# Residual adds, q rests, gradient stores and normalized-input stores moved between engines and queues in a one-core transformer-block backward kernel

## The chip, the cores and the metric

The kernel runs on one core of one Trainium2 chip. A core has TensorE (PE, matmuls and the loads of their stationary operand, PEld), VectorE (DVE), ScalarE (ACT), GpSimd (POOL) and SyncE (SP), each with an instruction stream of its own that runs in order, and DMA queues that SyncE, ScalarE and GpSimd issue to. The metric is the device time of one execution in microseconds (us); lower is better.

## The reference

One pre-norm block is run forward, and the gradients of all its inputs are taken. Everything is bf16, S = 2048 tokens, D = 640, H = 32 heads of 20, F = 1728.

```python
def _A_ref(x, wqkv, wo):                       # linear attention
    q, k, v = split_heads(x @ wqkv)
    phi = lambda t: jnp.where(t > 0, t + 1, jnp.exp(t)) + 1e-6
    pq, pk = phi(q), phi(k)
    kv = jnp.einsum("bhsd,bhse->bhde", pk, v)
    z = jnp.einsum("bhsd->bhd", pk)
    o = jnp.einsum("bhqd,bhde->bhqe", pq, kv) / (jnp.einsum("bhqd,bhd->bhq", pq, z)[..., None] + 1e-6)
    return join_heads(o) @ wo

def _B_ref(x, w1, w3, w2):                     # gated MLP
    return (silu(x @ w1) * (x @ w3)) @ w2

h = x + _A_ref(layernorm(x), wqkv, wo)
out = h + _B_ref(layernorm(h), w1, w3, w2)
# outputs: out, and the gradients of x, wqkv, wo, w1, w3, w2 for a given grad_out
```

## The kernel before, in words

Tokens are cut into 16 tiles of 128 rows (`t`), grouped four to a chunk of 512 (`c`); F is cut into 14 slices of 128 (`fc`), taken in pairs (`k`). The order of instructions on every engine is the order in which the Python code emits them (a manual schedule); the framework only adds the waits. Tile pools recycle their buffers, so a write to a recycled buffer waits for whatever still reads it. DMAs of one queue are handed out over eight semaphores in turn, so one also waits for the eighth before it.

The work goes through these stages:

1. **Start, about 0 to 78 us.** x is loaded and normalized tile by tile in place (`ln1`, `x_sb`); TensorE transposes the first eight tiles, and DMA transposes (`p1_norm`) make `pqT` for the others. Each tile gets k (`p1_mm`, `phi`) and some tiles q. The function phi is split: ScalarE computes exp and relu from the accumulator (`mq`, `rq`), and a held "rest" on VectorE (min, add, add) finishes it later (`phi_rest` runs held rests in order, leaving `keep` of them). A list `trickle` holds loads of weights, of which one is issued per tile; `group_out` stores a finished group of four k tiles (`pk_d`) and normalized x tiles (`xn_d`). `load_wq` loads 320 columns of wqkv per step, `load_w2T` loads w2 transposed, and `ghh_chunk` multiplies it with grad_out ahead of need.
2. **Attention output, about 78 to 107 us.** A hand-written list of steps (`run((q_late, 10, f2_mT), ...)`) interleaves: the last q tiles 10 to 15 (`q_late`), the product of kv and wo (`f2_wT`), the division by the denominator (`r_...`), the attention output plus the residual for tiles 0 to 4 (`f2_half(t, j)`, j being a half of 320 columns), the statistics of the second norm (`ln2.part`), the normalized tile (`f2_hn`) and its transpose on TensorE (`f2_ht`). By the time the residual is added, x_sb has been reloaded with x.
3. **Gated MLP, about 107 to 336 us.** For each chunk and slice, TensorE computes `ghh` (four slices ahead), gate and up; ScalarE moves them out of PSUM (L668 to L676); after every pair, seven VectorE products (`mlp_pair`, `op`) are queued in `later` and drained one at a time. Three of them are stored to DRAM by `store`: hh, and the gradients of gate and up (`gg_d`). The tiles sig, s2, gate and up have two buffers each, so ScalarE's copy into `up` of pair k + 2 waits until the store of pair k has landed. Side steps (`sides`, `r_steps`) compute the attention output of the next chunk and the scaled q rows (`r_load`, `r_den`, `r_end`).
4. **Gradients, from 355 us.** Weight gradients, input gradients and their norms; they read back what was stored.

`f2_at` adds the residual in one of two ways. For tiles 5 to 7, TensorE adds it with a matmul of the identity and x, and ScalarE copies the sum into x_sb; for all others, VectorE adds accumulator and x_sb:

```python
on_pe = TPC < t < 2 * TPC
...
    if on_pe:
        T.matmul(at[:, 0:HD], lhsT=ident[:], rhs=xs, start=True, stop=False)
...
    if on_pe:
        A.copy(out=xs, in_=at[:, 0:HD])
    else:
        V.tensor_tensor(out=xs, in0=at[:, 0:HD], in1=xs, op=ALU.add)
```

GpSimd computes the reciprocal square root of each variance (`ln_rs`, L152) and issues stores of the q rows (`r_d`, `pq_d`) and of a few small matrices.

Of the kernel before, what the change touches and what calls it, by code (L numbers as in the profile page):

```python
# [9 lines left out]
P = 128  # L10
BF16 = mybir.dt.bfloat16
F32 = mybir.dt.float32
ALU = mybir.AluOpType
# [11 lines left out]
HD = D // 2  # L25
# [30 lines left out]
def kernel(  # L56
# [116 lines left out]
    wqkv = U1.tile([P, DT, 3 * D], BF16, name="wqkv", tag="D")  # L173
    wq_v = A_wqkv.rearrange("(c p) n -> p c n", p=P)

    def load_wq(a, b, q=dma):
        q(out=wqkv[:, :, a * HD:b * HD], in_=wq_v[:, :, a * HD:b * HD])

    def load_x(a, b):
        dma(out=x_sb[:, a:b, :], in_=xS[:, a:b, :])  # L180

    load_x(1, 2)
    A.activation(sg[:], zero[:], AF.Exp)
    load_wq(2, 3, A.dma_start)
    load_wq(3, 4, A.dma_start)
    load_x(2, 3)
    load_x(3, 4)
    load_x(4, 6)
# [229 lines left out]
    load_w2T(0, 2 * P)  # L418
    load_x(6, 8)
    load_g2T(0)  # L420
    load_x(8, 12)
    load_wq(0, 2)
    load_x(12, ST)
# [10 lines left out]
        ln1.part(x_sb, t + 1, 0)  # L434
        p1_norm(t)
    ln1.part(x_sb, 3, 1)
    trickle += [lambda: load_w2T(2 * P, 4 * P), lambda: load_wq(4, 6)]
    for c0, c1 in ((0, 2), (2, 4), (4, 5)):
        trickle += load_w13(c0, c1)
    trickle += [lambda: dma(out=w1[:, :, F:FP], in_=rows(B_w3)[:, :, F - FL:F])]  # L440
# [4 lines left out]
    stat_of = {0: (4,), 1: (5,), 2: (6,), 3: (7,), 4: (8, 9), 5: (10,), 6: (11,), 7: (12, 13), 8: (14,), 9: (15,)}  # L445
    norm_of = {0: (3,), 1: (4,), 2: (5,), 3: (6,), 4: (7,), 5: (8, 9), 6: (10,), 7: (11,), 8: (12, 13), 9: (14,), 10: (15,)}

    def group_out(g):
        sl = slice(g * TPC, (g + 1) * TPC)
        dma(out=pk_v[:, sl, :], in_=pk_all[:, sl, :])  # L450
        dma(out=xn_v[:, sl, :], in_=x_sb[:, sl, :])

    QT = (5, 7, 9, 11)
    for t in range(ST):
# [98 lines left out]
    hn, hnT, hhT = {}, {}, {}  # L553

    def f2_at(t, tag="at", halves=(0, 1)):
        on_pe = TPC < t < 2 * TPC
        for j in halves:
            at = ps.tile([P, 512], F32, name="at", tag=tag, bufs=2)
            xs = x_sb[:, t, j * HD:(j + 1) * HD]
            if on_pe:  # L560
                T.matmul(at[:, 0:HD], lhsT=ident[:], rhs=xs, start=True, stop=False)
            for c in range(DT):
                T.matmul(at[:, 0:HD], lhsT=pqT[:, c, t * P:(t + 1) * P], rhs=Wp[:, c, j * HD:(j + 1) * HD],  # L563
                         start=(c == 0 and not on_pe), stop=(c == DT - 1))
# [3 lines that stand above are left out]
                V.tensor_tensor(out=xs, in0=at[:, 0:HD], in1=xs, op=ALU.add)  # L568
            ln2.part(x_sb, t, j)

    def q_late(t, between=None):

        mq, rq = (p1.tile([P, D], BF16, name=n, bufs=b) for n, b in (("mq", 3), ("rq", 3)))
        q_home(t)
        for j in range(2):
            acc = ps.tile([P, 512], F32, name="mm", bufs=4)
            js = slice(j * HD, (j + 1) * HD)
            p1_half(acc[:, 0:HD], t, j * HD)
            if j == 0 and between is not None:
                between()  # L580
            A.activation(mq[:, js], acc[:, 0:HD], AF.Exp)
            A.activation(rq[:, js], acc[:, 0:HD], AF.Relu)

# [21 lines left out]
    def f2_mT():  # L605
        tr = ps.tile([P, DT, P], BF16, name="trm", tag="at", bufs=2)
        for c in range(DT):
            T.transpose(tr[:, c, :], mbs[:, 0, c * P:(c + 1) * P], ident[:])
        A.copy(out=mT[:, :, (DT - 1) * P:], in_=tr[:])

    def q_out(a, b):
        src = pq6[:, 4:6, :] if a == 8 else pkx[0][:, DT + a - 10:DT + b - 10, :]
# [67 lines left out]
        if i == 1:  # L680
            mlp_pair(c, k, *pair.pop(k), ghh.pop(n // 2))

    def store(dst, r0, c, k, src):
        cs = slice(c * W, (c + 1) * W)
        r0 += k * 2 * P
        if k < FT // 2 - 1:
            dma(out=dst[r0:r0 + 2 * P, cs].rearrange("(i p) w -> p i w", p=P), in_=src)
        else:
            dma(out=dst[r0:r0 + P, cs], in_=src[:, 0, :])
            dma(out=dst[r0 + P:r0 + P + FL, cs], in_=src[:FL, 1, :])  # L690

    later = []

# [4 lines left out]
    def mlp_pair(c, k, sig, s2, gate, up, gh):  # L698

        hh = hhT[c][:, 2 * k:2 * k + 2, :]  # L700

        def op(out, a, b, alu=ALU.mult, to=None, r0=0):
            def go():
                V.tensor_tensor(out=out, in0=a, in1=b, op=alu)
                if to is not None:
                    store(to, r0, c, k, out)
            later.append(go)

        sig, s2, gate, up, gh = (x[:] for x in (sig, s2, gate, up, gh))
        op(gate, gate, sig)  # L710
        op(hh, gate, up, to=hh_d)
        op(s2, gate, s2)
        op(gate, gate, gh, to=gg_d, r0=F)
        op(s2, s2, sig, ALU.add)
        op(s2, s2, up)
        op(up, s2, gh, to=gg_d)

    def o2_steps(c, q=dma, tag="o2"):

# [33 lines left out]
    def run(*steps):  # L753
# [3 lines left out]
    Wp = U1.tile([P, DT, D], BF16, name="Wp", tag="MW")  # L757
    pkx.append(p1.tile([P, DT + 6, D], BF16, name="pkx", tag="pk"))
    run((q_late, 10, f2_mT), (f2_kv, 2), (f2_kv, 3), (f2_kv, 4), (phi_rest,), (q_late, 11), (f2_wT, 0), (f2_wT, 1),
        (phi_rest,), (q_late, 12), (f2_wT, 2), (f2_wT, 3), (f2_wT, 4), (phi_rest,), (q_late, 13),  # L760
        (r_red, 3), (r_inv, 3), (r_scale, 3), (r_prod, 5), (load_x, 2, 4), (r_T, 3), (q_late, 14), (r_red, 4),
        (r_inv, 4), (r_scale, 4), (r_T, 4), (load_x, 4, 8), (mlp_ghh, 4), (load_w2T, 8 * P, 10 * P), (q_late, 15),
        (sig_table,), (f2_half, 0, 0), (f2_half, 1, 0), (f2_half, 0, 1), (f2_half, 1, 1), (f2_hn, 0), (mlp_ghh, 5),
        (f2_half, 2, 0), (f2_hn, 1), (f2_m_out,), (load_w2T, 10 * P, 12 * P), (f2_half, 2, 1), (phi_rest, 2),
        (f2_ht, 0), (mlp_ghh, 6), (f2_half, 3, 0), (f2_hn, 2), (f2_w_out,), (f2_ht, 1), (f2_half, 3, 1), (phi_rest, 1),
        (mlp_ghh, 7), (f2_half, 4, 0), (f2_hn, 3), (phi_rest,), (q_out, 10, 16), (load_w2T, 12 * P, F), (f2_ht, 2),
        (f2_ht, 3), (f2_half, 4, 1), (r4_out,), (r_red, 5), (r_inv, 5), (r_scale, 5), (r_out, 5), (r4b_out,),
        (q_out, 8, 10))
    p1.release()
    pa = pool("pa", "right")  # L770

# [25 lines left out]
    def r_end(t):  # L797
# [1 line left out]
        r_out(t)  # L799

    r_steps = [{1: ((r_den, 6),), 2: ((r_end, 6), (r_load, 8)), 4: ((r_den, 7), (r_load, 9)), 5: ((r_end, 7),),
                12: ((r_load, 10),)},
               {0: ((r_den, 8),), 1: ((r_end, 8), (r_load, 11)), 2: ((r_den, 9),), 3: ((r_end, 9), (r_load, 12)),
                5: ((r_den, 10),), 6: ((r_end, 10), (r_load, 13)), 8: ((r_den, 11),), 9: ((r_end, 11), (r_load, 14)),
                11: ((r_den, 12),), 12: ((r_end, 12), (r_load, 15))},
               {0: ((r_den, 13),), 1: ((r_end, 13),), 3: ((r_den, 14),), 4: ((r_end, 14),), 6: ((r_den, 15),),
# [1 line left out]
    for c in range(SC):  # L808
        hhT[c] = pa.tile([P, FT, W], BF16, name="hhT", bufs=2)
        o2 = o2_steps(c - 1) if c > 0 else None  # L810

        def run_side(pos, fc):
            if c + 1 < SC:
                for f, i in sorted(sides[c][pos].get(fc, ()), key=lambda x: (x[0] is f2_ht, x[1])):
                    f((c + 1) * TPC + i)

        for fc in range(FT):
            mlp(c, fc, lambda: run_side(0, fc))
            drain(1)
            if o2 and not (c == SC - 1 and fc == 5):  # L820
                next(o2, None)
            run_side(1, fc)
            drain(1)
            if (c, fc) in ((0, 12), (1, 2)):
                load_x(8 + 4 * c, 12 + 4 * c)
            if c == 0 and fc in (5, 7, 9, 11):
                a, b = {5: (0, 3), 7: (3, 6), 9: (6, 10), 11: (10, 13)}[fc]
                dma(out=w2[:, a:b, :], in_=B_w2[a * P:b * P, :].rearrange("(c p) n -> p c n", p=P))
                if fc == 11:
                    dma(out=w2[0:FL, FT - 1, :], in_=B_w2[(FT - 1) * P:F, :])  # L830
            for f, t in r_steps[c].get(fc, ()):
                f(t)
# [569 lines left out]
```

## Time and profile before

| What | Value |
|---|---|
| time, median of 4 runs | 839.91 us (838.47 to 843.01) |
| profiled execution: time | 838.47 us |
| profiled execution: span, first to last instruction | 836.8 us |
| mean granted TensorE clock | 0.998 |
| TensorE busy | 820.7 us (98%) |
| VectorE busy | 456.3 us (55%) |
| ScalarE busy | 316.9 us (38%) |
| GpSimd busy | 79.7 us (10%) |
| mean DMA rate | 188 GB/s |

A row of the timeline gives the start and the time taken in us from the span's start, then the engine ("SPq" is SyncE's sequencer, which issues DMAs), the line in the kernel, the operation and the tiles; in brackets stands how long the engine was idle before it, and what released it. A row of the costliest groups gives the busy time, the mean of one in ns, and the idle time before them. TensorE is an in-order engine whose matmuls are pipelined: five of 320 columns take about 0.68 us, five of 512 about 1.08 us.

### The profile page before, as it was taken

Reading aid. Unit: us, or ns where it says so; the run is one execution under the profiler, and the core shown is the slowest. Engines: PE = TensorE matmul, PEld = TensorE weight load, DVE = VectorE, ACT = ScalarE, POOL = GpSimd, SP = SyncE. Lnnn points to the kernel's source line nnn. Section 1 sums busy time; section 2 is a strip of 40 time slices with the busy share of each in tenths; the row PEclk is TensorE's granted clock in tenths of the full one; section 3 lists DMA queues with packets and bytes.
Section 4 is the critical chain, followed back from the end, with each engine's and each line's share of the span. In section 5 each row is a group of like instructions: output and inputs, shape, how many; then the busy total and the mean of one; then the engine's idle time right before and its main releaser. Section 6 shows DMA issues by size and latency. Waiting matters only on the chain.

```text
span 836.8 us, 14163 instructions
## 1 busy us (share of the span) xinstructions
PE 820.7 (98%) x5548; PEld 523.9 (63%) x5548; DVE 456.3 (55%) x968; ACT 316.9 (38%) x599; POOL 79.7 (10%) x117
## 2 busy tenths in 40 slices
PE   8999899999999999999999999999999999999998
PEld 5667544455555555777777777777777777555554
DVE  7947988798998666500037777772681545200000
ACT  5755657755555666111122121222211433311111
POOL 2314221001010000000001111110110000000000
PEclk9999999999999999999999999999999999999999
DMA  9998978685585357799967788436998798876671
GB/s 265 261 350 148 219 238 216 205 226 152 144 202 156 111 162 219 205 240 226 287 159 178 191 188 209 96 89 124 207 243 173 162 190 178 214 186 149 158 172 37
DMA packets 330066, 157.58 MB, mean 188 GB/s; under 512 B 235344, under 2 KB 327152, under 8 KB 330000
## 3 DMA queue, kind: packets, MB, share of 16 engines
q1 hardware_dynamic: 302000, 136.61, 67.5%
q10 hardware_dynamic: 25728, 12.05, 6.7%
q0 software_dynamic: 2272, 8.03, 2.8%
q8 instruction: 43, 0.70, 0.4%
q14 instruction: 23, 0.19, 0.1%
HBM read 48.15 MB, written 51.46 MB: 119 GB/s over the span
## 4 chain that ended last, share of the span: by engine, by line
PE 88%; DVE 4%; DMA 3%; ACT 1%; SPq 1%; issue 1%; DVEq 0%; ACTq 0%
PE job L1167 19%; PE mm L364 19%; PE ghn L969 14%; PE o L728 7%; PE gxn L1326 7%; PE gw L922 7%; PE gwo L1054 3%; PE gr L1026 3%; PE macc L385 2%; PE dkv L1270 2%; PE big L255 2%; PE at L563 2%; DMA w2T<-in_B_w_dram 1%; DMA pqT<-x_sb 1%; DVE st L147 1%
## 5 line engine op out<-in xcount | busy, mean ns | idle before, releaser
L1167 PE MATMUL job<-gb,hnN 128*128 128x432 bf16 x640 | 117.0, 346 | 0.0
L969 PEld LDWEIGHTS <-ggb 128*128 128x128 bf16 x864 | 84.5, 98 | 32.8
L1167 PEld LDWEIGHTS <-hnN 128*128 128x128 bf16 x640 | 62.6, 98 | 54.1
L364 PE MATMUL mm<-pqT,w 128*128 128x512 bf16 x405 | 94.3, 381 | 0.0
L364 PEld LDWEIGHTS <-w 128*128 128x128 bf16 x540 | 53.1, 98 | 63.5 <-issue 0.8
L1171 ACT CAST obs<-job 128x432 bf16<-128x432 f32 (+1 forms) x60 | 29.1, 485 | 123.6 <-PE job L1167 121.2
L728 PE MATMUL o<-w,hhT 128*128 128x320 bf16 x448 | 67.5, 299 | 0.0
L364 PE MATMUL mm<-g2T,w2T 128*128 128x512 bf16 x260 | 64.6, 379 | 2.2 <-ACT up L676 2.2
L969 PE MATMUL ghn<-w13a,ggb 128*128 128x320 bf16 x448 | 63.5, 299 | 0.0
L969 PE MATMUL ghn<-w13b,ggb 128*128 128x320 bf16 x416 | 61.4, 299 | 0.0
L728 PEld LDWEIGHTS <-hhT 128*128 128x128 bf16 x448 | 43.8, 98 | 23.6
L922 PE MATMUL gw<-g,hb 128*128 128x320 bf16 x416 | 57.0, 299 | 0.0
L922 PEld LDWEIGHTS <-hb 128*128 128x128 bf16 x416 | 40.6, 98 | 15.7
L374 ACT CAST ghh<-mm 128x512 bf16<-128x512 f32 x52 | 30.6, 588 | 51.1 <-PE mm L364 48.5
L1326 PE MATMUL gxn<-wqT,gT 128*128 128x320 bf16 x320 | 48.9, 299 | 0.1
L1034 POOL TENSOR_TENSOR sz<-Zb,g_h 128x640 f32<-128x640 bf16 x16 | 20.2, 1261 | 270.7 <-issue 162.9
L364 PEld LDWEIGHTS <-w2T 128*128 128x128 bf16 x280 | 27.2, 98 | 28.8 <-issue 2.5
L668 ACT ACTIVATE sig<-mm 128x512 bf16<-128x512 f32 x56 | 33.6, 600 | 29.0 <-PE mm L364 26.5
L255 PE MATMUL big<-wqkv,pqT 128*128 128x320 bf16 x260 | 39.3, 299 | 3.0 <-ACT pqT L251 1.6
L981 ACT ACTIVATE gs<-ghn 128x640 bf16<-128x640 f32 x16 | 11.2, 703 | 78.6 <-PE ghn L969 78.6
L255 PEld LDWEIGHTS <-pqT 128*128 128x128 bf16 x320 | 30.4, 98 | 16.7 <-ACT pqT L251 2.5
L1326 PEld LDWEIGHTS <-gT 128*128 128x128 bf16 x320 | 31.2, 98 | 12.5 <-DMA gT<-g_k 0.4
(186 smaller groups left out, 1222.7 us busy)
## 6 DMA issues: line engine op xcount, KB each, us to landing
hh_d<-hhT SPq DMA_DIRECT2D x24, 256.0 KB, 2.4
gg_d<-gate SPq DMA_DIRECT2D x24, 256.0 KB, 3.0
gg_d<-up SPq DMA_DIRECT2D x24, 256.0 KB, 2.8
ggb<-gg_d SPq DMA_DIRECT2D x6, 896.0 KB, 5.9
ggb<-gg_d SPq DMA_DIRECT2D x6, 832.0 KB, 7.0
out_dram<-obs ACTq DMA_DIRECT2D x40, 108.0 KB, 2.5
ggb<-gg_d SPq DMA_DIRECT2D x2, 1728.0 KB, 12.7
x_sb<-in_A_x_dram SPq DMA_DIRECT2D x5, 640.0 KB, 5.8
```

What stands on the lines that cost most here:

```text
L255: T.matmul(acc, lhsT=pqT[:, c, t * P:(t + 1) * P], rhs=wqkv[:, c, n0:n0 + HD], start=(c == 0), stop=(c == DT - 1))
L364: T.matmul(acc[:], lhsT=w[:, c, fc * P:(fc + 1) * P], rhs=rhs[:, c, :], start=(c == 0), stop=(c == DT - 1))
L374: A.copy(out=ghh[n // 2][:, n % 2, :], in_=acc[:])
L668: A.activation(sig[:, i, :], gp[:], AF.Sigmoid)
L728: T.matmul(o2["ps"][:, 0:HD], lhsT=hhT[c][:, fc, i * P:(i + 1) * P], rhs=w2[:, fc, j * HD:(j + 1) * HD], start=(fc == 0), stop=(fc == FT - 1))
L922: T.matmul(acc[:, j, 0:HD], lhsT=hb[b][:, t, i * P:(i + 1) * P], rhs=g2[:, t, j * HD:(j + 1) * HD], start=(t == 0), stop=(t == ST - 1))
L969: T.matmul(acc[:, j, 0:HD], lhsT=ggb[t // 2][:, k, lo:lo + P], rhs=rhs[:, j * HD:(j + 1) * HD], start=(k == 0), stop=(k == NG - 1))
L1026: T.matmul(gr[t][:, j, 0:HD], lhsT=ghT[t][:, c, :], rhs=wT2[:, c, j * HD:(j + 1) * HD], start=(c == 0), stop=(c == DT - 1))
L1054: T.matmul(acc[m][:, j, 0:n], lhsT=r_sb[:, t, m * P:(m + 1) * P], rhs=g_hx[:, t, j * HD:j * HD + n], start=(t == 0), stop=(t == ST - 1))
L1167: T.matmul(acc[:, 0:n], lhsT=lhs[:, t, m * P:(m + 1) * P], rhs=rhs(t), start=(t == 0), stop=(t == ST - 1))
L1171: A.copy(out=ob, in_=acc[:, 0:n])
L1326: T.matmul(acc[:, j, 0:HD], lhsT=g, rhs=wqT[:, k, j * HD:(j + 1) * HD], start=(k == 0), stop=(k == 14))
```

## The change

There are five edits.

- `f2_at` decides per half: the residual of half j = 1 goes by the identity matmul for tiles below 4 as well. Tile 4 stays with VectorE.
- `q_late` for tiles 14 and 15 writes its exp and relu into a tile `qx` that takes the memory of wo, which is no longer needed then, and finishes in place there. Their rests are run by a new step `q_rest` at slice 4 of MLP chunk 1, which also stores both tiles to `pq_d`; `q_out` in the attention stage stores tiles 10 to 13 alone.
- The hand-written list of steps is reordered a little: `f2_wT(4)` runs between the halves of `q_late(13)`, and the last `phi_rest`, `q_out`, `f2_ht`, `mlp_ghh(7)` and `f2_half(4, 0)` change places.
- The store of the up gradient goes to GpSimd's queue; hh and the gate gradient stay on SyncE's.
- The stores of normalized x of groups 2 and 3 leave `group_out` and are issued by GpSimd in MLP chunk 0, slices 6 and 13; the reload of x_sb tiles 12 to 15 moves from slice 2 to slice 5 of chunk 1. At the start, all wqkv loads go by SyncE, and the second load of w2T leaves `trickle` and is issued ahead of the load of x tiles 8 to 11.

```diff
-    def load_wq(a, b, q=dma):
-        q(out=wqkv[:, :, a * HD:b * HD], in_=wq_v[:, :, a * HD:b * HD])
+    def load_wq(a, b):
+        dma(out=wqkv[:, :, a * HD:b * HD], in_=wq_v[:, :, a * HD:b * HD])
...
-    load_wq(2, 3, A.dma_start)
-    load_wq(3, 4, A.dma_start)
+    load_wq(2, 3)
+    load_wq(3, 4)
...
     load_g2T(0)
+    load_w2T(2 * P, 4 * P)
     load_x(8, 12)
...
-    trickle += [lambda: load_w2T(2 * P, 4 * P), lambda: load_wq(4, 6)]
+    trickle += [lambda: load_wq(4, 6)]
...
+    def xn_out(g, q):
+        sl = slice(g * TPC, (g + 1) * TPC)
+        q(out=xn_v[:, sl, :], in_=x_sb[:, sl, :])
+
     def group_out(g):
         sl = slice(g * TPC, (g + 1) * TPC)
         dma(out=pk_v[:, sl, :], in_=pk_all[:, sl, :])
-        dma(out=xn_v[:, sl, :], in_=x_sb[:, sl, :])
+        if g < 2:
+            xn_out(g, dma)
...
-        on_pe = TPC < t < 2 * TPC
         for j in halves:
+            on_pe = t < 2 * TPC and (t > TPC or (t < TPC and j == 1))
...
-        mq, rq = (p1.tile([P, D], BF16, name=n, bufs=b) for n, b in (("mq", 3), ("rq", 3)))
-        q_home(t)
+        if t < 14:
+            mq, rq = (p1.tile([P, D], BF16, name=n, bufs=b) for n, b in (("mq", 3), ("rq", 3)))
+            q_home(t)
+        else:
+            if t == 14:
+                qx.append(U1.tile([P, DT, D], BF16, name="qx", tag="W6"))
+            mq, rq = (qx[0][:, 2 * (t - 14) + i, :] for i in range(2))
+            pqs[t] = mq
...
+    def q_rest():
+        phi_rest()
+        dmaG(out=pq_v[:, 14:16, :], in_=qx[0][:, 0:4:2, :])
...
-    def store(dst, r0, c, k, src):
+    def store(dst, r0, c, k, src, q):
...
-            dma(out=dst[r0:r0 + 2 * P, cs].rearrange("(i p) w -> p i w", p=P), in_=src)
+            q(out=dst[r0:r0 + 2 * P, cs].rearrange("(i p) w -> p i w", p=P), in_=src)
...
-        op(up, s2, gh, to=gg_d)
+        op(up, s2, gh, to=gg_d, q=dmaG)
...
-        (phi_rest,), (q_late, 12), (f2_wT, 2), (f2_wT, 3), (f2_wT, 4), (phi_rest,), (q_late, 13),
+        (phi_rest,), (q_late, 12), (f2_wT, 2), (f2_wT, 3), (phi_rest,), (q_late, 13, lambda: f2_wT(4)),
...
-        (f2_half, 2, 0), (f2_hn, 1), (f2_m_out,), (load_w2T, 10 * P, 12 * P), (f2_half, 2, 1), (phi_rest, 2),
-        (f2_ht, 0), (mlp_ghh, 6), (f2_half, 3, 0), (f2_hn, 2), (f2_w_out,), (f2_ht, 1), (f2_half, 3, 1), (phi_rest, 1),
-        (mlp_ghh, 7), (f2_half, 4, 0), (f2_hn, 3), (phi_rest,), (q_out, 10, 16), (load_w2T, 12 * P, F), (f2_ht, 2),
-        (f2_ht, 3), (f2_half, 4, 1), (r4_out,), (r_red, 5), (r_inv, 5), (r_scale, 5), (r_out, 5), (r4b_out,),
-        (q_out, 8, 10))
+        (f2_half, 2, 0), (f2_hn, 1), (f2_m_out,), (load_w2T, 10 * P, 12 * P), (f2_half, 2, 1),
+        (f2_ht, 0), (mlp_ghh, 6), (f2_half, 3, 0), (f2_hn, 2), (f2_w_out,), (f2_ht, 1), (f2_half, 3, 1), (phi_rest, 2),
+        (q_out, 10, 14), (f2_ht, 2), (f2_hn, 3), (mlp_ghh, 7), (load_w2T, 12 * P, F), (f2_half, 4, 0), (f2_ht, 3),
+        (f2_half, 4, 1), (r4_out,), (r_red, 5), (r_inv, 5), (r_scale, 5), (r_out, 5), (r4b_out,), (q_out, 8, 10))
...
-                12: ((r_load, 10),)},
-               {0: ((r_den, 8),), 1: ((r_end, 8), (r_load, 11)), 2: ((r_den, 9),), 3: ((r_end, 9), (r_load, 12)),
+                6: ((xn_out, 2, dmaG),), 12: ((r_load, 10),), 13: ((xn_out, 3, dmaG),)},
+               {0: ((r_den, 8),), 1: ((r_end, 8), (r_load, 11)), 2: ((r_den, 9),), 3: ((r_end, 9), (r_load, 12)), 4: ((q_rest,),),
...
-            if (c, fc) in ((0, 12), (1, 2)):
+            if (c, fc) in ((0, 12), (1, 5)):
                 load_x(8 + 4 * c, 12 + 4 * c)
```

More of the change, by code (lines that the diff above doesn't have):

```diff
@@ L569, in f2_at @@
             ln2.part(x_sb, t, j)
+    qx = []
     def q_late(t, between=None):
-        mq, rq = (p1.tile([P, D], BF16, name=n, bufs=b) for n, b in (("mq", 3), ("rq", 3)))
-        q_home(t)
+        if t < 14:
[6 more added lines that the diff above has]
+            pqs[t] = mq
         for j in range(2):
@@ L686, in store @@
         if k < FT // 2 - 1:
-            dma(out=dst[r0:r0 + 2 * P, cs].rearrange("(i p) w -> p i w", p=P), in_=src)
+            q(out=dst[r0:r0 + 2 * P, cs].rearrange("(i p) w -> p i w", p=P), in_=src)
         else:
-            dma(out=dst[r0:r0 + P, cs], in_=src[:, 0, :])
-            dma(out=dst[r0 + P:r0 + P + FL, cs], in_=src[:FL, 1, :])
+            q(out=dst[r0:r0 + P, cs], in_=src[:, 0, :])
+            q(out=dst[r0 + P:r0 + P + FL, cs], in_=src[:FL, 1, :])
     later = []
@@ L700, in mlp_pair, with op @@
         hh = hhT[c][:, 2 * k:2 * k + 2, :]
-        def op(out, a, b, alu=ALU.mult, to=None, r0=0):
+        def op(out, a, b, alu=ALU.mult, to=None, r0=0, q=dma):
             def go():
@@ L705, in go @@
                 if to is not None:
-                    store(to, r0, c, k, out)
+                    store(to, r0, c, k, out, q)
             later.append(go)
@@ L830 @@
                     dma(out=w2[0:FL, FT - 1, :], in_=B_w2[(FT - 1) * P:F, :])
-            for f, t in r_steps[c].get(fc, ()):
-                f(t)
+            for f, *t in r_steps[c].get(fc, ()):
+                f(*t)
             if c == 2 and fc == 3:
```

## The prediction

> **What bounds the kernel now.** I read the page's busy times first, then TensorE's chain of waits, then the timeline where those waits stand.
>
> ```profile
> PE 820.7 (98%) x5548; PEld 523.9 (63%) x5548; DVE 456.3 (55%) x968; ACT 316.9 (38%) x599; POOL 79.7 (10%) x117
> ```
>
> The chain of TensorE's waits (line, waited for: us in total, times, longest):
>
> ```profile
> PE trh L640 <- DVE hn L155: 3.9, 2, 3.0
> PE mm L364 <- ACT up L676: 2.2, 1, 2.2
> ...
> PE gp L364 <- DMA w2T<-in_B_w_dram: 1.0, 1, 1.0
> PE big L255 <- DMA pqT<-x_sb: 0.8, 1, 0.8
> ```
>
> TensorE is busy 820.7 of 836.8 us. Only what shortens its idle 16.1 us, or what is added to its work, can move the time. Two waits are large: 3.9 us behind VectorE's hn, and 2.2 us behind ScalarE's copy into `up`.
>
> ```profile
> 102.10:105.10 3.00, 0.01 (x1) 0.00 (x0) 2.79 (x9) 0.69 (x1) 0.56 (x1) 0.93 0.89 337
> 105.10:108.40 3.30, 3.29 (x15) 1.83 (x16) 1.82 (x5) 0.69 (x1) 0.87 (x1) 0.55 0.66 175
> ```
>
> Two stretches (time, then PE, PEld, DVE, ACT, POOL busy, granted clock, DMA). In the first TensorE does nothing and VectorE is 93% busy: VectorE is the bound from about 85.7 us to hn(3). In the second the granted clock is 0.55. So the wait of 3.0 us is paid a second time: at half clock, 3.3 us hold about 1.65 us of matmul.
>
> ```profile
> 119.71 0.69 DVE L704 TENSOR_TENSOR up<-s,ghh 128x1024 bf16<-128x1024 bf16 x1
> ...
> 120.09 0.57 POOL L358 DMA_DIRECT2D r_d<-pql  x1 [6.41 <-DVE pql L350]
> ...
> 121.75 0.40 SPq L687 DMA_DIRECT2D gg_d<-up  x1
> ...
> 125.98 0.58 ACT L676 CAST up<-mm 128x512 bf16<-128x512 f32 x1 [3.44 <-DMA gg_d<-up]
> ...
> 126.62 1.24 PE L364 MATMUL mm<-g2T,w2T 128*128 128x512 bf16 x5 [2.20 <-ACT up L676]
> ```
>
> The second wait: `up` of pair 0 is finished at 120.40, but its store is issued at 121.75, behind a transpose and a load in SyncE's queue; it lands at 125.88 (4.13 us), ScalarE may then overwrite the tile, and TensorE resumes at 126.62.
>
> **The change part by part.**
>
> *Residuals and q rests.* The rows (busy, mean ns, idle before):
>
> ```profile
> L568 DVE TENSOR_TENSOR x_sb<-at,x_sb 128x320 bf16<-128x320 f32 x26 | 12.5, 482 | 5.1 <-PE at L563 5.1
> ...
> L566 ACT CAST x_sb<-at 128x320 bf16<-128x320 f32 x6 | 2.7, 465 | 0.6 <-PE at L563 0.6
> ...
> L561 PE MATMUL at<-x_sb,ident 128*128 128x320 bf16 x6 | 1.8, 299 | 0.0
> ```
>
> The condition covers four halves (tiles 0 to 3, j = 1), not five: tile 4 meets neither branch. VectorE's timeline from the first L568 (91.85) to the end of hn(3) (105.05) is 13.2 us without a gap that matters. Out of it go four L568, 0.52 from start to start: 2.1. Tile 14's rest (L585, L586: 102.86 to 103.69) goes: 0.8. The add and statistics of tile 4's first half (103.69 to 104.62) now come after hn(3): 0.9. VectorE's own chain becomes 13.2 - 3.8 = 9.4 us. It also starts 0.35 earlier, since tile 12's rest no longer waits behind wT(4) (VectorE idles 0.49 there at 85.73).
>
> By that VectorE would finish at 100.9; but then TensorE and ScalarE bind. TensorE from at(0,0) at 90.69: ten attention halves at 0.68, four identity matmuls at 0.14 (starts 116.15 to 116.29), three ghh chunks at 1.08, four transposed tiles at 0.37 = 6.8 + 0.56 + 3.24 + 1.5 = 12.1, to 102.8. Following each release, I find two stops: at(3,0) ends at 98.5, then bn, hn(2), ScalarE's copy of (3,1) at 99.8 to 100.25 (0.47), its statistics, tile 13's rest (0.8, kept), and hn(3) ends at 102.4, so trh(2) and trh(3) wait about 0.5 together; ScalarE's copy of trh(3) ends at 103.6. The MLP starts at 103.7 instead of 106.95: 3.25 gained, the identity matmuls paid. ScalarE's 1.28 us table load at 91.67 delays copy (0,1) to 93.16, and costs VectorE 0.35 there, which it can spare. No gap near 3 us remains, so the half clock goes as well; before the MLP that is in the 3.25, and from 106.95 to 108.4 it is half of 1.45 = 0.75 more. Together 4.0. Bounds: 2.0 (copies late) to 4.9 (TensorE never waits).
>
> The two rests (two of 0.32 and 0.49, 1.6 us) go to MLP chunk 1, step 4, just ahead of an `up` product near 179.6. VectorE is idle 0.97 before the next pair there, and TensorE has four accumulators of lead; I take 0. Without that cover: 1.6. The data stay in wo's tile, which wT(4) has finished with; the reload of tiles 14 and 15 is at steps 9 and 12 of that chunk, at least 15 us after the new store.
>
> *Up stores on GpSimd.* 24 large stores and 4 split ones leave SyncE's queue. GpSimd has no row for 128x2x512. Its 160 KB stores in the MLP (`r_d<-pql`) take 0.54 to 0.58 to issue and 3.0 to 4.5 to land, 3.1 in the middle; its 320 KB store 0.74 and 3.9. For 256 KB I take 0.65 and 3.6. Behind each in GpSimd's queue stand ln_rs (a later product of VectorE, so already late enough) and r_d stores; r_load waits for those at least one step later.
>
> Take G, the end of gate(1) on ScalarE (112.53 before). VectorE is full from G until `up` is done at G + 7.9. Before, TensorE ran dry at G + 11.85 and resumed at G + 14.1. Now: r_d of tile 6 is issued until G + 8.15, the store lands at G + 11.75, ScalarE's copy takes 0.6, TensorE resumes at G + 12.45: the stop is about 0.55 instead of 2.2, gain 1.7. Some is given back: the next store ends 128.47 + 0.1 + 3.3 to 3.6 = about 132, while ScalarE, now 1.7 earlier, asks at 129.1 (it asked at 130.76). TensorE's lead over ScalarE there is 2.4 to 3.3, so I charge 0.4. Net 1.3; bounds 0 to 2.2. Later pairs: from VectorE's end to ScalarE's next use are 3.5 to 4.9 us in chunks 0 and 1, about the 3.7 that a store takes; the waits of 1.4 and 2.4 us that ScalarE has before at 187.0 and 161.6 cost TensorE nothing, so a small excess is covered.
>
> *The rule against it.* The Trainium skill, "SBUF — State Buffer", section "SBUF: two separate sides" and the one after it, says that VectorE and GpSimd lock one shared pair of ports, so that VectorE's two-port modes keep GpSimd from writing descriptors; it tells of a DMA of 0.62 us that took 3.1 us so. That would add 2.5: landing at 6.1, the first stop 2.95 instead of 0.55, and some 1 us more at the next pairs: about 3 us worse. The row decides for 3.6: the same queue's stores landed in 3.0 to 4.5 with VectorE 94% busy. The lock does show in ln_rs, 0.87 to 0.93 in the MLP against 0.56 ahead of it.
>
> *Loads and xn stores.* Ahead of about 40 us VectorE is full and DMA is too. The wqkv halves move behind x(1) on SyncE; x(1) lands sooner than its 5.19, but VectorE next needs x(2), and x(0..2) plus both halves are 1.31 MB at the 300 GB/s of that stretch: 4.4 + 2.8 = 7.2, as now (7.14). The w2T load ahead of x(8..11) ends the 1.0 us wait of gp, which VectorE hides anyway. x(8..11) then land near 16.9, and VectorE needs them at 18.89. But the trickle is one item ahead: w3's first 0.85 MB (3 us) now stands before pqT(8), the first stores and pqT(10), where DMA had room at 32 to 36 us.
>
> ```profile
> 36.65 2.89 SPq L242 DMA_TRANSPOSE pqT<-x_sb  x2
> ...
> 44.64 1.53 PE L255 MATMUL big<-wqkv,pqT 128*128 128x320 bf16 x10 [0.82 <-DMA pqT<-x_sb]
> ```
>
> That wait ends with the second of these transposes, 6.65 us after its issue at 37.95; I put it 0.6 to 1.1 later, and TensorE has no slack from there to 78 us. I charge 0.8 (bounds: 0.8 gained to 2.0 lost). The two late xn stores (0.66 MB each, GpSimd, chunk 0 at steps 6 and 13) leave a full queue at 44 to 60 us where TensorE does not wait, and precede their overwriting loads by six steps: 0; uncovered, some 2.3 us of DMA each.
>
> **Sum.** 3.25 + 0.75 + 1.3 - 0.8 = 4.5. The profiled execution took 838.47 (span 836.8 and 1.7 around it), so its like is 834.0; it is the fastest of the four runs, whose median is 839.91, so I forecast 835.4.
>
> **Rivals.** (a) All goes well: no loss at the start, TensorE never waits for `up`: 3.25 + 0.75 + 2.2 = 6.2, and the 0.8 us wait gone: 7.0, so 832.9. For it: both waits are near their ends. (b) Descriptors are starved as the skill's page says: 838.4. Against it, the landings quoted. (c) ScalarE is late with the four copies behind table load and ghh casts, the lower bound of 2.0: 837.4. Against it: ScalarE is busy 5.2 of 13.3 us there. (d) The w2T transpose holds SyncE's queue for 5.0 us, as the same transpose did at 12.53; x(8..11) are issued at 16.5 and land near 22, 3 us after VectorE needs them: 838.4. Against it: at 12.53 three loads stood ahead of that transpose, now none. (e) The other side: up stores slower than the buffers bear. With 4 us from VectorE's end to ScalarE's use and 3 of TensorE's lead, landing beyond some 7 us stops TensorE at each pair; at 8 us that is 1 us in 24 pairs: 839.9 - 4.0 + 0.8 + 24 = 861. Against it: 4.5 was the longest.
>
> **How the numbers follow.** Forecast 0.58, own range 833.4 to 837.4; (a) 0.12; (b) 0.08; (c) 0.08; (d) 0.04; (e) 0.10. Half a per cent, about what a measurement of this kernel can tell, puts the bound at 835.7: two thirds of the forecast's case and (a) lie below, 0.39 + 0.12 = 0.51 faster; (e) 0.10 slower; the rest 0.39. The range 832.0 to 839.6 takes in (a) to (d).
>
> **What would show it.** Right: trh waits for hn under 1 us; granted clock 1.0 in the MLP's first 3 us; MLP matmuls from about 104; the wait for `up` under 1.2; `gg_d<-up` from GpSimd landing at 3.2 to 4.2; the wait for pqT near 45 us at 1 to 2. Wrong: TensorE waiting for ScalarE's `x_sb` copies or for `up` more than once, landings over 6, or VectorE waiting for x_sb near 19 us.

## The result and the profile after

The changed kernel takes 837.61 us (median of 43 runs, 835.02 to 840.54) against 839.54 us for the kernel before (64 runs). The ratio is 0.9971, 95% interval 0.9963 to 0.9979: 2.4 us faster, with an interval of 1.8 to 3.1 (the two medians alone differ by 1.9). The forecast was 4.5 us, to 835.4, with 833.4 to 837.4 as the range of its own case; the measured time lies 0.2 us above that range.

The two profiled executions do not show this difference: the one before is a quick one of its kernel (838.47), the one after a slow one (838.87), and their spans are 836.8 and 837.2 us. So the profiles are compared stage by stage here, and times are taken from the medians.

| us | start to first attention half (L563, after L569) | from there to first MLP matmul | MLP, to first `gw` matmul | from there to the end |
|---|---|---|---|---|
| before | 90.68 | 16.27 | 247.89 | 481.91 |
| after | 90.23 | 14.82 | 250.71 | 481.40 |

The MLP starts at 105.05 instead of 106.95: 1.90 gained. Of these, 0.45 came before the first attention half; the stretch behind it, for which 3.25 had been forecast, became 1.45 shorter. Then the MLP is 2.8 us longer. Busy times of the changed kernel:

```profile
PE 820.3 (98%) x5552; PEld 522.9 (62%) x5552; DVE 453.8 (54%) x964; ACT 317.8 (38%) x603; POOL 103.8 (12%) x152
```

VectorE has 2.5 us of work less, GpSimd 24 us more, and TensorE is as busy as before. Its waits in the changed kernel (line, waited for: us in total, times, longest; `trh` is the transpose of hn, `mm` at L364 a product of the MLP):

```profile
PE trh L658 <- DVE hn L155: 2.7, 1, 2.7
PE mm L364 <- ACT up L694: 2.4, 4, 1.1
PE big L255 <- ACT pqT L251: 1.6, 2, 0.8
PE mm L364 <- DMA pqT<-hn: 1.5, 1, 1.5
PE big L255 <- DMA pqT<-x_sb: 1.3, 3, 0.8
```

The wait for hn only fell from 3.9 to 2.7. The wait for `up` is no smaller: one stop of 2.2 became four that sum to 2.4. And one wait is new, 1.5 us for `pqT<-hn`. The timeline of the changed kernel shows what stands behind each. First, the entry to the MLP:

```profile
94.63 2.45 SPq L413 DMA_TRANSPOSE w2T<-in_B_w_dram  x1
...
94.92 0.44 DVE L155 TENSOR_SCALAR hn<-x_sb,ln_mv,ln_rs 128x640 bf16<-128x640 bf16 x1
...
97.18 1.02 SPq L646 DMA_DIRECT2D hn_d<-hn  x2
...
101.28 0.45 DVE L155 TENSOR_SCALAR hn<-x_sb,ln_mv,ln_rs 128x640 bf16<-128x640 bf16 x1 [2.22 <-DMA hn_d<-hn]
...
101.78 0.45 PE L658 MATMUL trh<-ident,hn 128*128 128x128 bf16 x5 [2.69 <-DVE hn L155]
```

hn has two buffers, so hn(2) may be written only when the store of hn(0) has landed. hn(0) is ready at 95.36, but SyncE is in a transposing load of w2T from 94.63 and issues the store at 97.18; it lands at 101.2. VectorE, which has its work done early now, waits 2.22 us for it. Before the change the store was issued as soon as hn(0) was written, landed at 100.90, and hn(2) started at 101.16:

```profile
96.41 0.44 DVE L155 TENSOR_SCALAR hn<-x_sb,ln_mv,ln_rs 128x640 bf16<-128x640 bf16 x1
...
96.88 1.61 SPq L628 DMA_DIRECT2D hn_d<-hn  x2
...
101.16 0.43 DVE L155 TENSOR_SCALAR hn<-x_sb,ln_mv,ln_rs 128x640 bf16<-128x640 bf16 x1
```

So the store was done 0.26 us before VectorE came to hn(2), and no row showed it as a wait.

Second, the third `up` store of MLP chunk 0, same view:

```profile
132.23 0.69 DVE L722 TENSOR_TENSOR up<-s,ghh 128x1024 bf16<-128x1024 bf16 x1
...
132.59 0.79 POOL L451 DMA_DIRECT2D xn_d<-x_sb  x1
133.48 0.71 POOL L705 DMA_DIRECT2D gg_d<-up  x1
139.31 0.58 ACT L694 CAST up<-mm 128x512 bf16<-128x512 f32 x1 [4.15 <-DMA gg_d<-up]
139.94 1.24 PE L364 MATMUL mm<-g2T,w2T 128*128 128x512 bf16 x5 [0.50 <-ACT up L694]
...
140.25 0.89 DVE L147 BATCH_NORM_STATS2 st<-x_sb 128x6 f32<-128x320 bf16 x2 [3.43 <-ACT x_sb L572]
```

One of the two moved xn stores is issued just ahead of an `up` store, which then lands after 5.73 us. ScalarE waits 4.15 us for the buffer; behind its copy of `up` in ScalarE's order stands a residual copy (L572), so VectorE waits 3.43 us for that. TensorE itself stops three more times, by 0.50, 0.28 and 0.55 us. At the boundary of chunks 1 and 2 it stops again, same view:

```profile
215.29 0.44 DVE L155 TENSOR_SCALAR hn<-x_sb,ln_mv,ln_rs 128x640 bf16<-128x640 bf16 x1
...
216.87 1.24 SPq L654 DMA_TRANSPOSE pqT<-hn  x1
...
221.23 2.33 PE L364 MATMUL mm<-pqT,w 128*128 128x512 bf16 x10 [1.47 <-DMA pqT<-hn]
```

The half clock at the start of the MLP is gone in this execution (stretch; PE, PEld, DVE, ACT and POOL busy; granted clock; DMA share and rate):

```profile
99.10:101.78 2.68, 0.00 (x1) 0.01 (x1) 0.50 (x2) 0.42 (x1) 0.00 (x0) 1.00 1.18 350
...
105.05:108.35 3.30, 3.30 (x16) 1.53 (x16) 3.09 (x9) 2.02 (x4) 1.30 (x2) 1.00 0.92 317
```

### The profile page after: what moved, and what is told of

It is laid out like the page before. It is cut to its first block, busy times and chain, and to the rows that moved or that the text cites. A ratio compares the mean times of both kernels' runs of the same rounds, so it can differ in the third digit from the quotient of the medians.

```text
span 837.2 us, 14175 instructions
## 1 busy us (share of the span) xinstructions
PE 820.3 (98%) x5552; PEld 522.9 (62%) x5552; DVE 453.8 (54%) x964; ACT 317.8 (38%) x603; POOL 103.8 (12%) x152
## 4 chain that ended last, share of the span: by engine, by line
PE 84%; DMA 6%; DVE 6%; ACT 2%; issue 1%; SPq 0%; POOL 0%; DVEq 0%; ACTq 0%; POOLq 0%
PE job L1184 19%; PE mm L364 15%; PE ghn L986 14%; PE gxn L1343 8%; PE gw L939 7%; PE o L746 5%; PE gwo L1071 3%; PE dkv L1287 3%; PE gr L1043 3%; PE big L255 2%; PE macc L385 2%; DMA gg_d<-up 2%; DMA pqT<-x_sb 2%; PE at L569 1%; DVE st L147 1%
## 5 line engine op out<-in xcount | busy, mean ns | idle before, releaser
L364 PE MATMUL mm<-pqT,w 128*128 128x512 bf16 x405 | 93.9, 379 | 1.9 <-DMA pqT<-hn 1.5
L364 PEld LDWEIGHTS <-w 128*128 128x128 bf16 x540 | 52.7, 98 | 65.6 <-DMA pqT<-hn 2.0
L364 PE MATMUL mm<-g2T,w2T 128*128 128x512 bf16 x260 | 64.6, 379 | 2.4 <-ACT up L694 2.4
L364 PEld LDWEIGHTS <-w2T 128*128 128x128 bf16 x280 | 27.2, 98 | 28.2 <-issue 3.5
L255 PEld LDWEIGHTS <-pqT 128*128 128x128 bf16 x320 | 30.3, 98 | 17.8 <-DMA pqT<-x_sb 2.8
```

The costliest lines, as they stand in the source:

```text
L255: T.matmul(acc, lhsT=pqT[:, c, t * P:(t + 1) * P], rhs=wqkv[:, c, n0:n0 + HD], start=(c == 0), stop=(c == DT - 1))
L364: T.matmul(acc[:], lhsT=w[:, c, fc * P:(fc + 1) * P], rhs=rhs[:, c, :], start=(c == 0), stop=(c == DT - 1))
```

## The experiments

The working theory (A in the expectations): two waits that the prediction had not seen eat the gain, the store behind hn's two buffers (1.8 to 2.2 us) and the late xn stores (2 to 3 us). The rivals: the lead is spent at the chunk boundary whatever its source, or the GpSimd stores of `up` are what costs. Ratios are to the kernel before on the same chip, with 95% intervals. A difference of two ratios is given with the root of the sum of their squared half-widths.

**The w2T load behind hn(0)'s store.**

```diff
-(load_w2T, 8 * P, 10 * P), (q_late, 15), ... (f2_hn, 0), (mlp_ghh, 5),
+(q_late, 15), ... (f2_hn, 0), (load_w2T, 8 * P, 10 * P), (mlp_ghh, 5),
```

> The changed kernel with one step moved: the transposing load of w2T columns 8P to 10P is issued after the store of hn(0) instead of before q_late 15. Theory A (SyncE held hn(0)'s store behind that load, so hn(2), which reuses hn(0)'s buffer, came late): hn(0)'s store is issued at about 95.4 us instead of 97.18 and lands about 99.4 instead of 101.2, VectorE's wait before hn(2) falls from 2.22 to under 0.6 us, TensorE's wait for hn at trh falls from 2.7 to under 1.2, and the first MLP matmul comes about 1.8 us earlier, at 103.3. If that lead is kept to the end: ratio to before 0.995 (-4.2 us). If it is spent at the boundary of MLP chunks 1 and 2, where TensorE waits for the transposes of hn (theory B): the wait pqT<-hn grows from 1.5 to about 3 us and the ratio stays at 0.997. Theory C (the store lands late because the rings are full, wherever it is issued): landing about 101 again, wait at trh 2.5 or more, ratio 0.997.

Measured: 834.07 us, ratio 0.9959 (0.9942 to 0.9976), which is 0.0012 +- 0.0019 below the changed kernel and not clear of noise. The trace shows the mechanism: the store is issued at 95.48 and lands at 99.60, VectorE waits 0.54, TensorE 1.0, and the stretch to the MLP falls from 14.82 to 13.14 us. Theory A holds for the entry, and C falls. The wait for `pqT<-hn` does not grow (1.3), so it does not take the lead back, as B had it.

**The side work of chunk 1 one block earlier.**

```diff
-            k0 = 3 * i - (i == TPC - 1) + (-2, 1, 0)[c]
+            k0 = 3 * i - (i == TPC - 1) + (-2, 0, 0)[c]
```

> The changed kernel with one number changed: the side work of MLP chunk 1 (second residual, hn and its transposing load for tiles 8 to 11) runs one feature block, about 4.7 us, earlier. Theory B (the lead is spent at the boundary of chunks 1 and 2 because TensorE arrives there before the transposes of hn have landed): the 1.5 us wait of TensorE for pqT<-hn near 220 us disappears and the time falls by 1.2 to 1.5 us against the changed kernel, ratio to before 0.9955. Theory D (VectorE is the limit of that stretch, 9.6 us busy of 10, so the same work earlier only moves the stop): a stop of the same size appears elsewhere between 170 and 225 us, ratio 0.997.

Measured: 845.5 us, ratio 1.0076 (1.0055 to 1.0096). Neither theory had this. The wait for `pqT<-hn` is gone, but another is in its place, in the list of TensorE's waits of this kernel:

```profile
PE at L569 <- DMA pqT<-pql: 7.4, 2, 3.8
```

The attention halves of tiles 8 to 11 need the scaled q rows, whose transposes are made in the same slices. One block earlier they are not there. The boundary can't be eased by this shift.

**The up stores back on SyncE.**

```diff
-        op(up, s2, gh, to=gg_d, q=dmaG)
+        op(up, s2, gh, to=gg_d)
```

> The changed kernel with the stores of the up gradient issued by SyncE again; all else kept. By the prediction's sum (the GpSimd stores gain 1.3 us net): slower than the changed kernel by about 1.3 us, ratio to before 0.9987, with the first stop of TensorE before ScalarE's copy of up back at about 2.2 us. By what the changed kernel's trace shows instead (one stop of 2.2 us became four that sum to 2.4): no difference within 0.5 us, ratio 0.997. If the GpSimd stores are themselves what costs time in the MLP (rival: their landings of up to 6.9 us hold the up buffers): faster by about 1 us, ratio 0.996.

Measured: 836.82 us, ratio 0.9981 (0.9965 to 0.9997); against the changed kernel 0.0010 +- 0.0018 higher. TensorE's largest wait for `up` is 1.0, not 2.2, so the size of the first stop does not hang on the queue. The rival, that the stores on GpSimd themselves cost time, is not seen. The wait of 1.5 us for `pqT<-hn` is there as in the changed kernel, and one of 1.6 for `gate` is new. Its timeline shows that the late xn stores do harm here too, though no `up` store stands behind them in GpSimd's queue:

```profile
129.57 0.79 POOL L451 DMA_DIRECT2D xn_d<-x_sb  x1
129.97 0.37 SPq L705 DMA_DIRECT2D gg_d<-up  x1
134.29 0.59 ACT L694 CAST up<-mm 128x512 bf16<-128x512 f32 x1 [1.92 <-DMA gg_d<-up]
...
137.54 0.79 POOL L451 DMA_DIRECT2D xn_d<-x_sb  x1
...
149.54 0.59 ACT L688 CAST gate<-mm 128x512 bf16<-128x512 f32 x1 [2.80 <-DMA gg_d<-gate]
```

The `up` store beside the first xn store lands 4.22 us after its issue, from SyncE's queue.

**All xn stores in the first phase.**

```diff
-        if g < 2:
-            xn_out(g, dma)
+        xn_out(g, dma)
...
-                6: ((xn_out, 2, dmaG),), 12: ((r_load, 10),), 13: ((xn_out, 3, dmaG),)},
+                12: ((r_load, 10),)},
```

> The changed kernel with all four xn stores issued by SyncE in the first phase again (none in the MLP). By the prediction the moved stores cost and gain nothing: ratio 0.997, unchanged. By the trace of the changed kernel, the xn store issued at 132.58 us lies on GpSimd's queue just ahead of the up store issued at 133.47, which lands 5.73 us later instead of about 3; ScalarE then waits 4.15 us for the buffer and TensorE stops three times by 0.5 us. Without it those stops fall from 1.3 to about 0.3 us: the MLP gains 1.0 us, and if the first phase loses nothing the ratio is 0.996; if the stores delay loads of the first phase instead, the net phase ends later than 78.7 us and the ratio is 0.997 to 0.998.

Measured: 833.53 us, ratio 0.9940 (0.9919 to 0.9961): 2.6 +- 1.9 us less than the changed kernel, more than the 1.0 expected. The same `up` store now lands 2.99 us after its issue. Of TensorE's waits from the entry on, only two over 0.2 us are left, and one in the MLP:

```profile
PE trh L657 <- DVE hn L155: 2.7, 1, 2.7
...
PE mm L364 <- ACT up L693: 1.1, 1, 1.1
```

The three smaller stops and the wait for `pqT<-hn` are both gone, and the MLP takes 246.19 us instead of 250.71. I had not counted the second: the stop at 221 us is a late effect of the store at 133. Counted from the MLP's start, VectorE writes the hn of the last tile of chunk 1 at 37.76 us in the changed kernel and at 35.01 here, 2.75 apart; it is still 2.52 apart at the last tile of chunk 2 (110.24 and 107.72), whose transpose TensorE then waits for. The second xn store, at 155, adds next to nothing (2.87 at the next tile). The first phase is not longer: the first attention half comes at 88.45 instead of 90.23.

**Both repairs, and the up stores on SyncE with early xn stores.** The first joins the edits of the first and fourth experiment, the second those of the third and fourth.

> The changed kernel with both repairs: all xn stores in the first phase, and the w2T load of columns 8P to 10P behind hn(0)'s store. If the two losses are separate (one at the entry to the MLP, one in its first chunk), the gains add: first matmul of the MLP 18.5 to 19 us after the first attention half, as with the load moved alone, against 14.8 in the changed kernel read at the same marks less 1.6; MLP (its first matmul to the first gw matmul) 246 us; ratio to before 0.994 less 0.0012 to 0.002, that is 0.992 to 0.993. If the lead is taken back somewhere later in the MLP whatever its source, the MLP grows to 247.5 and the ratio stays at 0.994.

> The changed kernel with the up stores on SyncE and all xn stores in the first phase: beside the run with only the xn stores in the first phase it tells what the up stores on GpSimd are worth where no xn store stands ahead of them. By the prediction's sum, 1.3 us: ratio to before 0.9955, a stop of TensorE of 2.2 us before ScalarE's copy of up near 12 to 20 us into the MLP, MLP 247.5 us long instead of 246.2. If GpSimd's stores gain nothing: ratio 0.994, MLP 246.2. If they cost (landings of 4 to 7 us): ratio 0.993, MLP 245.

Measured: 834.65 us, ratio 0.9947 (0.9927 to 0.9966), and 834.99 us, ratio 0.9944 (0.9924 to 0.9964). The first is not seen to be better than the early xn stores alone (0.0007 +- 0.0029 higher), though the interval leaves room for the gain of 0.0012 to 0.002 that was expected. The timeline of its profiled execution (837.24 us, above the median) shows what can take the gain away:

```profile
95.39 0.34 SPq L645 DMA_DIRECT2D hn_d<-hn  x1
95.78 2.70 SPq L413 DMA_TRANSPOSE w2T<-in_B_w_dram  x1
...
98.57 0.53 SPq L645 DMA_DIRECT2D hn_d<-hn  x1
...
104.57 0.45 DVE L155 TENSOR_SCALAR hn<-x_sb,ln_mv,ln_rs 128x640 bf16<-128x640 bf16 x1 [2.35 <-DMA hn_d<-hn]
```

hn(0)'s store is early, but now the load, which holds SyncE for 2.70 us here (1.68 in the first experiment), stands before hn(1)'s store, and hn(3) waits for that. In this execution the wait moved to a later tile. By the second, up stores on GpSimd are worth 0.0004 +- 0.0029 where no xn store is near. And beside the third experiment it gives the price of the late xn stores with the up stores on SyncE: 3.1 +- 2.1 us, with an MLP of 249.63 us against 246.53; the `up` store that took 4.22 us there takes 2.51 here. Counted from the MLP's start, SyncE issues the first one at 14.51 us and it lands at 17.57; GpSimd issues it at 13.48 and it lands at 17.23, because its landing takes 3.75 instead of 3.06. The stops are 1.4 and 1.1.

**The start-up loads as before, and the residual halves on VectorE again.**

```diff
+    load_wq(2, 3, A.dma_start)
+    load_wq(3, 4, A.dma_start)
-    load_wq(2, 3)
-    load_wq(3, 4)
...
-    load_w2T(2 * P, 4 * P)
...
-    trickle += [lambda: load_wq(4, 6)]
+    trickle += [lambda: load_w2T(2 * P, 4 * P), lambda: load_wq(4, 6)]
```

```diff
-            on_pe = t < 2 * TPC and (t > TPC or (t < TPC and j == 1))
+            on_pe = TPC < t < 2 * TPC
```

> The changed kernel with the loads of the first 20 us as before (two wqkv parts from ScalarE, the w2T part 2P to 4P in the trickle). The prediction charged the new order 0.8 us, between a gain of 0.8 and a loss of 2.0: then this kernel is faster than the changed one by 0.8, ratio 0.9961, net phase ending (first trm) about 0.8 earlier. Traces so far show TensorE's first matmul 0.5 us earlier with the new order (5.5 to 5.8 against 6.0), x(1) landed at 3.55 instead of 5.19, and the end of the net phase at 76.7 or 78.7 in kernels whose first phase is the same instruction for instruction, so the execution decides more than the order: then the ratio is 0.997 to 0.9985, first tr matmul at 6.0.

> The changed kernel with the four residual halves (tiles 0 to 3, second half) added on VectorE again. By the prediction's sum (VectorE bounds the entry to the MLP, four adds of 0.52 us are 2.1): MLP starts 2.1 us later, plus up to 0.75 of half clock: ratio 0.9996 to 1.0005. By the trace of the changed kernel (VectorE stands idle 2.22 us ahead of hn(2) until hn(0)'s store has landed): three of the four adds only fill that idle time, hn(2) starts as late as before, and the MLP starts 0.5 us later: ratio 0.9977.

Measured: 837.99 us, ratio 0.9990 (0.9977 to 1.0003), and 836.10 us, ratio 0.9965 (0.9949 to 0.9980). The new order of loads is thus not a loss of 0.8 us but a gain of 1.6 +- 1.3. Put the other way, with the old loads the change is not clear of the kernel before. And the residual halves, for which the forecast had the largest part of its gain, are not seen to be worth anything in the changed kernel: without them the ratio is 0.0006 +- 0.0017 lower. VectorE has 2.22 us to wait in any case, and the adds fill most of that time: the stretch to the MLP is 15.09 us without the halves, against 14.82. In the MLP a stop of 2.17 us for `up` and half clock behind it come in place of the four stops and the wait for `pqT<-hn`; the losses do not add. The q rests and the new order of steps were not undone by themselves.

**hn(2) in a buffer of its own.** The q rests use four of the five parts of `qx`; hn(2) goes into the fifth. Then hn(2) waits for no store, and hn(3) for that of hn(0).

```diff
-        hn[t] = pf.tile([P, D], BF16, name="hn", bufs=2)
+        hn[t] = qx[0][:, 4, :] if t == 2 else pf.tile([P, D], BF16, name="hn", bufs=2)[:]
```

It was run in the changed kernel, with the early xn stores, and with these once more without the residual halves and once without the new start-up loads.

> The changed kernel with only hn(2) given its own buffer; the late xn stores stay on GpSimd in the MLP. It tells whether the lead won at the entry to the MLP survives a MLP that is delayed by the late xn stores. If the two are separate: stretch to the MLP 13 us as in the kernel with both, MLP 249.5 to 250.7 us as in the changed kernel, ratio 0.9942 to 0.995 (2 us below the changed kernel). If an earlier MLP loses more to the late stores: MLP 252, ratio 0.997.

> The changed kernel with all xn stores in the first phase, and with hn(2) written to the free fifth part of the tile that holds the two q rests, so that hn(2) waits for no store and hn(3) reuses hn(0)'s buffer. Theory A (at the entry to the MLP the change's gain is eaten by a store: hn has two buffers, and hn(2) and hn(3) wait for the stores of hn(0) and hn(1), which SyncE issues behind transposing loads): VectorE's wait ahead of hn(2) (2.2 to 2.3 us) goes, TensorE waits under 1 us for hn at trh, the stretch from the first attention half to the first MLP matmul falls from 14.8 to 16.7 us (as executions differ) to 12.7 to 13.3, the granted clock stays at 1.0 there, and since the runs of xn in the first phase alone were spread between 832.2 and 836.5 by just this stretch, the ratio to before is 0.990 to 0.992. Rival: VectorE is the bound behind that wait, so only some 0.5 us is gained: stretch 14.3, ratio 0.9935.

> As the kernel with xn stores in the first phase and hn(2) in its own buffer, but the four residual halves (tiles 0 to 3, second half) added on VectorE again. With the wait for the store gone, VectorE should bound the stretch, as the prediction had it: three of the four adds stand ahead of hn(2) and one ahead of hn(3), so hn(3) comes 2.1 us later and the MLP starts 1.6 to 2.1 us later than in that kernel: ratio 0.0020 to 0.0025 higher. Rival: TensorE or ScalarE bind there, and the adds cost under 0.5 us: ratio within 0.0006.

> As the kernel with xn stores in the first phase and hn(2) in its own buffer, but with the loads of the first 20 us as in the kernel before. It measures the start-up term alone in a kernel where nothing later takes a lead back. By the prediction (the new order loses 0.8 us): ratio to before 0.9907, net phase ending 0.8 us earlier. By the profiles so far (first tr matmul at 6.0 to 6.1 with the old order against 5.5 to 5.8, 25.6 to 25.8 us from the fiftieth big matmul to the first macc ones against 24.9 or 26.7, a wait of 1.0 to 1.6 us of gp for w2T): the new order gains 1.4 us on average: ratio 0.9934, net phase ending at 78.6 to 79.6 instead of 76.9 to 77.1.

| kernel | us | ratio to before | to attention half | to MLP | MLP |
|---|---|---|---|---|---|
| changed + own buffer | 834.07 | 0.9950 (0.9936 to 0.9963) | 90.58 | 12.70 | 249.02 |
| changed + own buffer + early xn | 831.10 | 0.9917 (0.9903 to 0.9930) | 88.60 | 13.03 | 246.17 |
| the last, residual halves on VectorE | 835.47 | 0.9963 (0.9951 to 0.9976) | 88.43 | 14.30 | 249.14 |
| the last but one, start-up loads as before | 833.01 | 0.9941 (0.9927 to 0.9954) | 90.54 | 12.84 | 246.82 |

The two repairs add, as far as the intervals tell: the buffer gives 1.8 +- 1.3 us in the changed kernel and 1.9 +- 2.1 beside early xn stores; the xn stores give 2.8 +- 1.6 and 2.6 +- 1.9. With both, the kernel is 7.0 us faster than before, better than either given kernel. TensorE's waits in it:

```profile
PE mm L364 <- ACT up L693: 0.8, 1, 0.8
...
PE trh L657 <- DVE qx L155: 0.4, 1, 0.4
PE trh L657 <- DVE hn L155: 0.3, 1, 0.3
```

In that kernel the residual halves are worth 3.9 +- 1.5 us, where nothing was seen of them in the changed one. 1.3 of it is the stretch to the MLP. The rest is seen in the stretches of the kernel without the halves (columns as above):

```profile
119.50:122.05 2.55, 0.14 (x2) 0.00 (x1) 2.52 (x6) 0.64 (x2) 0.00 (x0) 0.98 0.89 268
122.05:125.45 3.40, 3.40 (x9) 1.20 (x9) 2.92 (x8) 2.91 (x6) 0.75 (x1) 0.52 0.55 72
```

The stop before the first copy of `up` grows from 0.8 to 2.4 us, and half clock follows it. The store is issued 13.48 us into the MLP in both kernels, but lands after 5.10 instead of 3.47 us. The other kernel with the halves on VectorE shows the same (4.85, and the stop of 2.17), while in the nine traces with the halves on TensorE and this store on GpSimd it lands after 3.47 to 4.16. Why, stays open.

## Why the prediction was right or wrong

- **Entry to the MLP, 3.25 forecast, 1.45 seen in the profile.** The step that failed is "Following each release, I find two stops". I followed engines, not buffers: hn has two, and the store that frees the first landed only 0.26 us before hn(2) began. VectorE's chain did become shorter; the store then decided. With that wait removed the stretch is 12.70 to 13.03 us, a gain of 3.2 to 3.6 against the 16.27 of before. So the mechanism and size were right, and one limit behind it was missed, at a price of 1.8 us. Rival (c) had the number that came nearest, 837.4, but of its mechanism nothing is seen: TensorE never waits for ScalarE's residual copies there.
- **Half clock, 0.75.** Right in the profiled execution, where the clock is 1.00 there, but only in part for the kernel: it is a matter of the execution. Of 65 executions of the kernel before that were run beside the experiments, 48 had a mean granted clock below 0.999, and still 25 of 44 of the changed one (the profiled one included), whose stop of 2.7 us remained; with hn(2) in its own buffer, none of 14 in the three kernels that keep the halves. In the changed kernel, those below took 838.1 us in the median, the others 836.5. The mean clock does not tell where in the kernel the half clock fell.
- **Late xn stores, forecast 0.** The step that failed is "leave a full queue ... where TensorE does not wait, and precede their overwriting loads by six steps: 0". They cost 2.6 to 2.8 us with the `up` stores on GpSimd and 3.1 +- 2.1 with them on SyncE. I looked at what the store itself must precede, not at the stores that free buffers beside it. The `up` store behind it in GpSimd's queue took 5.73 us instead of 2.99, and landed 1.1 us after the xn store had (138.13). But an `up` store on SyncE's queue at the same place took 4.22 instead of 2.51. So standing in the same queue is not needed for the delay; whether it adds to it is not shown.
- **Up stores on GpSimd, forecast 1.3.** Not measurable: 0.3 +- 2.4 us with early xn stores, 0.8 +- 1.5 with late ones. The issue is 1.0 us earlier, as worked out, and 0.72 us long in the median against the 0.65 taken. The error is in the landing: I set 3.6 for GpSimd against the 4.13 that SyncE's store took before, and SyncE's took only 3.06 when it was put back. The median landing from GpSimd is 3.0 us, the longest 6.9. Rival (b) is not seen: the second `up` store landed in 2.68 us with VectorE busy 9.76 of 10 us around it. VectorE's work there is for the most part TENSOR_TENSOR (about 7 of the 10 us), so this says little of other operations. Nor is (e) seen: landings near 7 us came singly, and the four stops sum to 2.4. Two of the prediction's own signs of being wrong did come, a landing over 6 us and more than one wait for `up`. The first was no good sign: the same store (at 155.03) took 6.45 us from SyncE before the change.
- **Start-up, forecast a loss of 0.8.** The wrong sign. It gains 1.6 +- 1.3 in the changed kernel and 2.0 +- 1.6 in the best one. I charged the trickle that is one item ahead and set the 1.0 us wait of gp for w2T at nothing, "which VectorE hides anyway"; put back, that wait is 1.4 to 1.6 us, and the first transposes start at 6.0 to 6.1 instead of 5.5 to 5.8. Which of these carries the gain was not separated. Rival (d) fell: x(8..11) landed at 19.23, later than the 16.9 forecast, but VectorE waited 0.10 us for them, not 3.
- **The q rests, forecast 0 in the MLP.** Not tested alone, but nothing speaks against it: with early xn stores chunk 1 takes 64.90 us (first to first gate matmul of chunks 1 and 2), as the 64.89 before.

Two terms were too good (1.8 and 2.7), one too bad by 2.8, and the up stores too good by about 1; 4.5 - 1.8 - 2.7 + 2.8 - 1.0 = 1.8, against 2.4 measured. The four figures come from different kernels and carry 1.3 to 2.4 us of noise each. That the change came out faster was in good part luck: the gain clear of noise came from the start-up loads, the one part that was forecast as a loss, while the residual halves and the up stores, forecast as gains, showed none clear of noise in this kernel.

## What to carry to other kernels

When a change frees an engine, look for what is ready just before the engine was: each buffer that its next write reuses, and when the transfer that frees it lands, even where the trace shows no wait there. A transfer moved to a quiet queue and a quiet stage is not free: look for the stores beside it, in any queue, whose landing frees a buffer. The delay of one such store can surface 90 us later as a wait of something else. An edit that shows no worth when undone in a kernel may be worth 3.9 us once the waits beside it are gone.

## What the runs showed of the hardware

**Half clock after short stops, or not.** In the kernel with the old start-up loads a stop of 2.41 us was followed by this:

```profile
99.90:102.40 2.50, 0.09 (x2) 0.01 (x1) 0.56 (x3) 0.43 (x2) 0.00 (x0) 0.97 1.17 343
102.40:106.00 3.60, 3.60 (x15) 1.91 (x16) 1.81 (x6) 1.28 (x2) 1.35 (x2) 0.55 1.03 373
```

while after a stop of 2.69 us the changed kernel's clock stayed at 1.00. A stop of 2.17 us (residual halves on VectorE) was followed by 3.5 us at 0.51, one of 2.20 us, at 126.62 in the kernel before, by full clock. In the clock records of the traces each of these stretches is 3.41 us long at 0.50, whatever the stop; with TensorE busy throughout, that is about 1.7 us of work lost. The Trainium skill, "TensorE: Matmul & The Clock Gate", Part 1, says that activity is watched in a window of about 3.4 us that runs freely. The length of the stretches agrees, and a free-running window would fit stops of like length with different ends; but the page names an idle window of about 3.4 us as the condition, and here 2.2 us were enough. Where the windows begin, no run shows.

**One program, two lengths of a phase.** Kernels whose first phase is the same instruction for instruction (all those with late xn stores and the new load order) took 24.84 to 24.91 us in two profiled executions from the fifty-first `big` matmul to the forty-first `macc`, and 26.67 to 26.91 in four; in three of the long ones the first transpose, issued at 24.5 to 25.0 us, lands at 32.0 to 32.5 instead of 30.3 to 30.4, and TensorE waits for `pqT<-x_sb` three times. So a difference of 2 us between two profiles says nothing by itself.

**A transposing load holds SyncE.** The w2T loads of the attention stage took from 1.2 to 3.2 us to issue, where most stores of hn took 0.3 to 0.6. A store that is ready meanwhile is issued only after the load: hn(0)'s at 97.18 behind a load that ended at 97.08 in the changed kernel, at 95.48 with the load behind it. What makes such a load long or short, the runs do not show.
